# Whole float32 scores in the first twelve heads of an attention-and-mixer kernel, instead of the first eight

## The chip, the cores and the metric

The kernel runs on one core of one Trainium2 chip. The metric is device microseconds of one execution, the median of several. Five engines have queues of their own: PE (TensorE, matmuls), DVE (VectorE), ACT (ScalarE), POOL (GpSimd), and SP (SyncE), which here only issues DMAs. Each queue runs in order, so an instruction that waits holds up all behind it on its engine; engines meet through semaphores.

## The reference, cut to what matters

```python
# q, k, v: (8 batches, 8 heads, 576 tokens, 64), float32
scores = scale * np.matmul(q, k.transpose(0, 1, 3, 2))
scores = np.where(block_i >= block_j, scores, -1e9)      # blocks of 64 tokens
attn = softmax(scores)                                   # with 1e-9 added to the sum
x = attn @ v                                             # -> (8, 576, 512)
u = x + ((x.transpose(0, 2, 1) @ U) @ V).transpose(0, 2, 1)   # U: 576x32, V: 32x576
out = u + np.maximum(u @ w_ch1, 0.0) @ w_ch2             # 512 -> 2048 -> 512
```

The weights U, V, w_ch1 and w_ch2 are float64 and come as pairs of 32-bit words.

## The kernel before

**Stages.** The attention runs head by head, 64 heads (8 batches of 8), numbered 0 to 63. Two heads make a pair; after each pair `mix` projects the pair's columns through U and V, and after four pairs a batch's u is complete. The channel mixer is cut in two halves of 1024 hidden columns. The first half (`ffn_chunk`, 16 chunks of 288 tokens, L465 and L488) is laid between the heads' work wherever PE has room, and what is left of it runs after the last head. The second half (`block_products`, L659) runs after that, alone. The first two chunks belong to batch 0 and are run in two turns, since the second half of their weights comes later. A chunk needs its batch's u, and the weights w1 and w2 of the first half, which come in 16 pieces of 128x512.

**Float32 products.** Most matmuls split an operand into a float32r high part and a rest and multiply the parts. The scores of heads from FS on are made like this: `split_qk` fetches q and k into `raw` twice (rows 0 to 63 and 64 to 127), ACT makes q1 and k1 (high parts, L877 and L878), POOL subtracts for the rest of q (L880), DVE for the rest of k (L885), and a DMA copies the high part of q to the lower rows of q2 (L892). Each tile of scores is then two float32r matmuls, L935 (q1, k1) and L936 (q2, k2). Heads below FS fetch q and k once, ACT scales k in place (L874), and each tile of scores is one whole float32 matmul of `raw` (L931), which the profile records in two halves. Rows 64 to 127 of `raw` hold the block mask as a product of two constant matrices; for the split form DVE casts them into q2 and k2 at heads FS - 2 and FS - 1 (L867). A head has five tiles of scores, of 64, 192, 320, 448 and 576 keys (the last as two of 288, in the bank `bw`). After them come the maximum (L949, DVE), exponentials (L960, ACT), inverse sums (L976, L977, DVE), normalising (L986, POOL), transposes on PE (L1019), and the product with v (L1061 in heads below FP = 10, L1077 in split form from there on).

**Weights.** A weight piece is fetched (L372, L387), takes an absolute value on ACT (L353), four DVE instructions (L331, L332, L337, L345), a cast on ACT (L360) and a subtraction on POOL (L361).

**What sets the order.** `Plan` collects all work as tasks with an engine, a cost in ns, a priority and dependencies. `issue` walks a model of the five engines in time and, whenever an engine is free in the model, issues its ready task with the smallest priority. A head h has priorities around 1000 h, its `split_qk` 900 earlier than the head before, the mixer's matmuls 1,000,000 and more; the weight pieces have numbers that put them between certain heads. So a changed cost or task anywhere changes the order of everything behind it, on all engines. Semaphores then keep the program right whatever the real times are. The costs that the plan gives to a head's scores:

```python
        if h < FS:
            add("PE", sum(1.667 * n for n in ns) / 2, pr, products, [raw], [bank])
        else:
            add("PE", _pe(*ns, m=ms), pr, products, [q1, k1, q2, k2], [bank])
```

Of the kernel before, what the change touches and what calls it, by code (L numbers as in the profile page):

```python
# [43 lines left out]

FP = 10

FS = 8

PB = (1, 1, 1, 2, 2)

# [87 lines left out]
class Plan:  # L138
# [8 lines left out]
    def add(self, engine, ns, prio, fn, reads=(), writes=(), hold=(), after=0, port=False):  # L147

        n = len(self.tasks)
        deps = set()  # L150
        for b in reads:
            deps.update(b.writers)
            b.readers.append(n)
        for b in hold:
            deps.update(b.readers, b.writers)
        for b in writes:
            deps.update(b.readers, b.writers)
            b.writers, b.readers = [n], []
        deps.discard(n)
        slots = {b for b in (*reads, *writes) if b.pool is not None}  # L160
        for b in slots:
            b.users += 1
        self.tasks.append((engine, ns, prio, fn, deps, after, slots, port or engine == "POOL"))
# [91 lines left out]
def attention_then_mixer(  # L255
# [599 lines left out]
    def split_qk(h, pr):  # L855
        raw, q1, k1, q2, k2 = (r[h % 2] for r in (raw_r, q1_r, k1_r, q2_r, k2_r))

        def fetch():
            nc.sync.dma_start(out=raw[0:64, :], in_=qk[h])
            if h >= FS:  # L860
                nc.sync.dma_start(out=raw[64:P, :], in_=qk[h])

        if h in (FS - 2, FS - 1):

            for n, (x, o) in enumerate(((q2, 0), (k2, S))):
# [3 lines left out]
                )  # L869
        add("SP", 1640 if h >= FS else 820, pr, fetch, writes=[raw], after=DL)  # L870
        if h < FS:
            add(
# [36 lines left out]
    def softmax(h, tiles, pr):  # L909
# [14 lines left out]
        def products():  # L924
            for i, at in parts:
                qs = slice(P * i + 64 - (P if i else 64), P * i + 64)
                for j in range(2 if wide else 1):
                    o = bank[:, j, :T] if wide else view(i, at)
                    ks = slice(j * T, j * T + T) if wide else slice(0, P * i + 64)
                    if h < FS:  # L930
                        nc.tensor.matmul(  # L931
# [7 lines left out]
        for i in tiles:  # L939
            ns += [T] * 4 if wide else [P * i + 64] * 2  # L940
            ms += [P if i else 64] * (4 if wide else 2)
        if h < FS:
            add("PE", sum(1.667 * n for n in ns) / 2, pr, products, [raw], [bank])
# [294 lines left out]
```

## Time and profile before

| what | before |
|---|---|
| median of 3 runs | 1201.78 us (1198.8 to 1202.18) |
| the profiled execution's own time | 1201.04 us |
| its span, first to last instruction | 1199.2 us |
| mean granted TensorE clock | 0.996 |
| first head's scores | 5.3 us |
| first split scores (head 8) | 77.3 us |
| first mixer matmul (L465) | 103.5 us |
| projection of heads 14 and 15 | 198.7 and 199.7 us |
| last projection (heads 62 and 63) | 676.5 us |

The profile is of one execution. Busy times of engines are sums over instructions; on PE, a matmul's recorded time runs from its start to a modelled end and overlaps with the next one's, so what a matmul costs in a stream is the distance from its start to the next start.

### The profile page before, as it was taken

The numbers are of one execution on the slowest core, as the hardware profiler recorded it, in microseconds if no ns is written. First come the engines' busy times: TensorE is split into PE (matmuls) and PEld (weight loads), VectorE is DVE, ScalarE is ACT, GpSimd is POOL, SyncE is SP. The second block draws the span as 40 slices with busy tenths as digits, with TensorE's granted clock in tenths as the row PEclk, the third lists the DMA queues.
The fourth block names the chain that finished last, engine by engine and source line by source line (L and its number), as shares of the span: only waits on it lengthen the run. The fifth ranks groups of instructions, "written<-read, shape, count | busy, mean of one in ns | idle before, by whom it ended". The sixth has DMA issues, their size and how long they took to land.

```text
span 1199.2 us, 25106 instructions
## 1 busy us (share of the span) xinstructions
PE 1169.1 (97%) x8970; PEld 1123.6 (94%) x8970; DVE 980.7 (82%) x2061; ACT 734.0 (61%) x1822; POOL 426.3 (36%) x588
## 2 busy tenths in 40 slices
PE   7989998999999999999999999999999999999998
PEld 5657888999999999999999999999999999999998
DVE  6879899888988898888887488425989889889887
ACT  6878686777878787878786344213544544544443
POOL 4558766665656566665654112210000000000000
PEclk9999999999999999999999999999999999999999
DMA  4465656535364535354532343211231231231221
GB/s 127 146 172 155 188 166 166 139 97 156 81 171 108 144 104 153 101 158 106 144 98 70 104 147 111 81 54 49 72 119 49 72 119 49 72 119 60 60 80 40
DMA packets 76428, 132.13 MB, mean 110 GB/s; under 512 B 9040, under 2 KB 53072, under 8 KB 76304
## 3 DMA queue, kind: packets, MB, share of 16 engines
q1 hardware_dynamic: 76304, 130.53, 38.8%
q8 instruction: 71, 1.16, 0.4%
q14 instruction: 53, 0.43, 0.1%
HBM read 92.75 MB, written 29.49 MB: 102 GB/s over the span
## 4 chain that ended last, share of the span: by engine, by line
PE 79%; DVE 11%; ACT 4%; issue 2%; DMA 2%; SPq 0%; POOL 0%; ACTq 0%; DVEq 0%; POOLq 0%
PE bb L659 29%; PE bf L465 10%; PE bf L488 10%; PE ba L1019 7%; PE ba L1077 5%; PE bg L465 4%; PE bg L488 4%; DVE mx L949 2%; DVE pl L1038 2%; ACT p L960 2%; PE ba L935 2%; PE ba L936 2%; PE ba L1061 1%; PE ba L1116 1%; PE ba L1102 1%
## 5 line engine op out<-in xcount | busy, mean ns | idle before, releaser
L986 POOL TENSOR_SCALAR p<-p,rv 128x192 f32<-128x192 f32 (+4 forms) x320 | 181.0, 580 | 150.5 <-DVE rv L977 92.7
L659 PE MATMUL bb<-hh,w1l 128*128 128x288 f32 x704 | 170.1, 295 | 0.0
L659 PE MATMUL bb<-hh,w1h 128*128 128x288 f32 x704 | 169.4, 295 | 0.0
L960 ACT ACTIVATE p<-ba,mx 128x448 f32<-128x448 f32 (+3 forms) x248 | 114.3, 466 | 22.2 <-DVE mx L949 18.9
L1019 PE MATMUL ba<-ident,p 128*128 128x128 f32 x768 | 123.5, 275 | 2.2 <-DVE pw L994 0.7
L1038 DVE TENSOR_TENSOR pl<-ba,ph 128x512 fp32r<-128x512 f32 x216 | 114.0, 550 | 11.7 <-ACT ph L996 9.2
L659 PE MATMUL bb<-hl,w1h 128*128 128x288 f32 x576 | 123.0, 295 | 0.1
L659 PEld LDWEIGHTS bb<-hh,w1l 128*128 128x128 f32 x704 | 122.9, 190 | 0.0
L659 PEld LDWEIGHTS bb<-hh,w1h 128*128 128x128 f32 x704 | 121.9, 188 | 0.0
L488 PE MATMUL bf<-hh,w2h 128*128 128x288 f32 x392 | 121.2, 309 | 0.0
L488 PE MATMUL bf<-hl,w2h 128*128 128x288 f32 x392 | 116.4, 297 | 0.0
L488 PE MATMUL bf<-hh,w2l 128*128 128x288 f32 x392 | 115.6, 295 | 0.0
L996 ACT CAST ph<-ba 128x512 fp32r<-128x512 f32 x216 | 100.5, 493 | 23.1 <-PE ba L1019 18.3
L447 POOL TENSOR_TENSOR ul<-ur,uh 128x288 fp32r<-128x288 f32 x72 | 63.3, 907 | 129.7 <-PE bf L465 72.6
L613 ACT CAST hh<-hb 128x576 fp32r<-128x576 f32 x98 | 65.9, 672 | 60.6 <-PE bb L659 58.1
L949 DVE TENSOR_REDUCE mx<-ba 128x1 f32<-128x448 f32 (+3 forms) x248 | 94.1, 407 | 10.0 <-PE ba L936 5.4
L1019 PEld LDWEIGHTS ba<-ident,p 128*128 128x128 f32 x768 | 90.5, 141 | 7.9 <-issue 4.5
L880 POOL TENSOR_TENSOR q<-raw,q 64x576 fp32r<-64x576 f32 x56 | 82.6, 1475 | 29.1 <-issue 9.2
L659 PEld LDWEIGHTS bb<-hl,w1h 128*128 128x128 f32 x576 | 91.9, 188 | 0.4 <-DVE hl L614 0.4
L1077 PE MATMUL ba<-ph,vs 128*128 128x256 f32 (+3 forms) x432 | 90.7, 263 | 0.1
L465 PE MATMUL bf<-uh,w1l 128*128 128x288 f32 x392 | 80.8, 303 | 0.0
L488 PEld LDWEIGHTS bf<-hh,w2l 128*128 128x128 f32 x392 | 74.9, 191 | 0.2
(167 smaller groups left out, 3288.1 us busy)
## 6 DMA issues: line engine op xcount, KB each, us to landing
raw<-in_qk_dram SPq DMA_DIRECT2D x120, 288.0 KB, 4.4
st<-in_w_dram SPq DMA_DIRECT2D x32, 512.0 KB, 3.6
o_d<-ot SPq DMA_DIRECT2D x72, 144.0 KB, 2.1
vr<-in_v_dram SPq DMA_DIRECT2D x32, 320.0 KB, 3.4
ur<-u_d SPq DMA_DIRECT2D x64, 144.0 KB, 3.0
whole<-o_d SPq DMA_DIRECT2D x32, 288.0 KB, 3.2
out_dram<-whole SPq DMA_DIRECT2D x32, 288.0 KB, 2.2
ur<-u_d SPq DMA_DIRECT2D x30, 288.0 KB, 3.2
```

Source lines behind the costliest of these rows:

```text
L465: nc.tensor.matmul(ps[:, :T], w()[wn][:, k, fs], m[k].ap, start=(i == 0), stop=(i == len(ops) - 1))
L488: nc.tensor.matmul(ps[:, :T], w()[wn][:, f, ms], hs[f][x].ap, start=(i == 0), stop=(i == len(ops) - 1))
L613: add("ACT", _act(2 * T, True), E, lambda: nc.scalar.copy(h.ap, x[0]()), [x[1]], [h])
L659: nc.tensor.matmul(bank[:, i, :T], x()[:, w(k)], p.ap[:, k, :], start=first and n == 0, stop=last and n == len(ops) - 1)
L880: "POOL", 1380, pr, lambda: nc.gpsimd.tensor_sub(q1[64:P, :], raw[64:P, 0:S], f32(q1[64:P, :])),
L949: lambda i=i, at=at: nc.vector.tensor_reduce(out=mx[: P if i else 64, i : i + 1], in_=view(i, at), op=ALU.max, axis=AX.XY if wide else AX. ...
L960: nc.scalar.activation(out.rearrange("p (j k) -> p j k", j=2) if wide else out, view(i, at), AF.Exp, bias=mx[:rows, i : i + 1], accum_out= ...
L986: lambda x=x, rows=rows, i=i: nc.gpsimd.tensor_scalar(out=x, in0=x, scalar1=rv[:rows, i : i + 1], scalar2=1.0, op0=ALU.mult, op1=ALU.mult),
L996: add("ACT", _act(n), pr, lambda: nc.scalar.copy(out(), inp()), reads, writes)
L1019: nc.tensor.transpose(out=bank[:, a : a + P], in_=pt_r[i][h % PB[i]][:, j * P : (j + 1) * P], identity=perm.ap)
L1038: "DVE", _dve(m), pr, lambda: nc.vector.tensor_sub(pl[:, low], bank[:, :m], f32(ph[:, low])), [bank, bh], [bl]
L1077: nc.tensor.matmul(bank[0 : c.stop, a:n], vs[:, j, c], x[:, _at(g, j)], start=(i == 0), stop=(i == len(ops) - 1))
```

## The change

`FS`, the number of heads with whole float32 scores, goes from 8 to 12:

```diff
-FS = 8
+FS = 12
```

Heads 8 to 11 now take the branch `h < FS` in `split_qk` (one fetch, one ACT pass, nothing on POOL and DVE, no copy of q) and in `softmax` (five tiles of one whole float32 matmul each, the last one as two). The casts of the mask (L867) move from heads 6 and 7 to heads 10 and 11. The condition `h < 8` that picks the bank of the 448-key tile stays as it is. The tasks' costs change with the branch, and so the plan orders the program anew: PE has 3072 matmuls of the first mixer half in both, but 282 of them stood ahead of the second projection matmul of heads 14 and 15 before, and 312 now; ahead of the last projection 1860 before, and 1818 now.

On PE, the first mixer matmul and what stands just ahead of it, before (bank bf takes mixer products, ba scores and transposes; k_0, q_0 are the parts of head 10):

```order
L935 MATMUL ba_97<-k_0_147,q_0_145 128x320
L936 MATMUL ba_97<-k_0_128,q_0_126 128x320
L935 MATMUL ba_98<-k_0_147,q_0_145 128x192
L936 MATMUL ba_98<-k_0_128,q_0_126 128x192
L935 MATMUL ba_98<-k_0_147,q_0_145 64x64
L936 MATMUL ba_98<-k_0_128,q_0_126 64x64
L465 MATMUL bf_90<-uh_106,w1h_199 128x288
```

The same place now (p are a head's probabilities, xt a pair's columns):

```order
L1019 MATMUL ba_97<-swap,p_0_137 128x128
L1019 MATMUL ba_97<-ident,p_0_139 128x128
L1019 MATMUL ba_97<-ident,p_0_137 128x128
L1019 MATMUL ba_97<-ident,p_0_139 128x128 x2
L465 MATMUL bf_90<-uh_106,w1h_199 128x288
L465 MATMUL bf_90<-uh_107,w1h_199 128x288
```

The first mixer matmul has moved behind all of head 10's scores, the first two matmuls of head 11's, and transposes of probabilities that came after it before.

On DVE, the last step of the last of the 16 weight pieces (the L345 here), before (mx are maxima, ut the sums of a pair's projection):

```order
L1136 TENSOR_TENSOR ut_170<-ba_95,xt_163 128x288
L1045 TENSOR_TENSOR ph_158<-ba_98,ph_158 64x64
L331 TENSOR_SCALAR z_103<-z_103 128x512
L332 TENSOR_SCALAR z_103<-z_103 128x512
L1038 TENSOR_TENSOR pl_159<-ba_95,ph_157 128x256
L949 TENSOR_REDUCE mx_154<-bw 128x1
L337 SCALAR_TENSOR_TENSOR z_103<-st_101,z_103 128x512
L1085 TENSOR_TENSOR xt_164<-ba_98,tmp_161 64x256
L1038 TENSOR_TENSOR pl_159<-ba_95,ph_157 128x320
L345 SCALAR_TENSOR_TENSOR z_103<-st_101,z_103 128x512
```

And now:

```order
L1038 TENSOR_TENSOR pl_159<-ba_96,ph_157 128x256
L337 SCALAR_TENSOR_TENSOR z_103<-st_101,z_103 128x512
L1122 TENSOR_TENSOR t_0_167<-tz_168,t_0_167 32x128
L345 SCALAR_TENSOR_TENSOR z_103<-st_101,z_103 128x512
L1038 TENSOR_TENSOR pl_160<-ba_95,ph_158 128x512
L1085 TENSOR_TENSOR xt_164<-ba_96,tmp_162 64x320
L1136 TENSOR_TENSOR ut_170<-ba_98,xt_163 128x288
L1038 TENSOR_TENSOR pl_160<-ba_97,ph_158 128x448
```

The piece's last step was row 373 on DVE and is now row 345; it stood behind the projection sums (L1136) of heads 12 and 13 and stands ahead of them.

On SP, the first copy of q (L892) and its neighbours, before, for head 8 (u_d holds u, st a weight piece, vr v, in_qk the queries and keys):

```order
L387 DMA st_101<-in_w_dram 128x1024
L859 DMA raw_131<-in_qk_dram 64x1152
L861 DMA raw_131<-in_qk_dram 64x1152
L898 DMA vr_149<-in_v_dram 128x640
L372 DMA st_100<-in_w_dram 128x1024
L892 DMA q_0_126<-q_0_145 64x576
L859 DMA raw_130<-in_qk_dram 64x1152
```

And now, for head 12:

```order
L898 DMA vr_150<-in_v_dram 128x640
L387 DMA st_101<-in_w_dram 128x1024
L892 DMA q_0_126<-q_0_145 64x576
L859 DMA raw_130<-in_qk_dram 64x1152
L861 DMA raw_130<-in_qk_dram 64x1152
L859 DMA raw_131<-in_qk_dram 64x1152
```

The first copy has moved from head 8 to head 12; ahead of it stands one weight fetch and one of v, without the pair of fetches of the next head.

## Prediction

> **What bounds the kernel now.** I read the page first, then a table of windows by stage, then the instructions in order of time around the heads that change.
>
> The page's first lines and two of its slice lines (40 slices of 30 us):
>
> ```profile
> span 1199.2 us, 25106 instructions
> PE 1169.1 (97%) x8970; PEld 1123.6 (94%) x8970; DVE 980.7 (82%) x2061; ACT 734.0 (61%) x1822; POOL 426.3 (36%) x588
> PE   7989998999999999999999999999999999999998
> DVE  6879899888988898888887488425989889889887
> ```
>
> TensorE carries the kernel, but not evenly: it has gaps in the first seven slices, which is where heads 8 to 11 run. The windows, cut at the places I need (busy us of each engine, then the granted clock, DMA share, GB/s):
>
> ```profile
> 63.70:103.50 39.80, 33.24 (x205) 23.35 (x205) 30.70 (x66) 31.89 (x87) 24.77 (x29) 1.00 0.67 174
> 103.50:172.50 69.00, 65.34 (x517) 62.95 (x515) 64.28 (x147) 52.23 (x143) 49.23 (x61) 0.98 0.61 172
> 172.50:200.00 27.50, 22.20 (x157) 19.64 (x156) 25.83 (x60) 19.48 (x54) 18.13 (x24) 0.88 0.53 148
> 200.00:660.00 460.00, 457.05 (x3777) 445.67 (x3777) 391.76 (x1017) 360.16 (x1032) 277.18 (x397) 1.00 0.47 124
> 700.00:1150.00 450.00, 449.86 (x3389) 449.63 (x3388) 358.68 (x539) 186.92 (x306) 18.25 (x18) 1.00 0.27 82
> ```
>
> From 200 us on PE is idle 3 us in 460, and after the attention not at all; 450 us hold 3389 products of 288 columns, 0.133 us each. Between 63.7 and 200 us it is idle 6.6 + 3.7 + 5.3 = 15.5 us, and runs at half clock for 2% of 69 us and 12% of 27.5 us, which loses 1.4 + 3.3 = 4.7 us: 20.2 us in all. DVE is busy 93% and 94% of the second and third window. So whatever is done to PE after 200 us shows in full; up to there DVE shares the pace, and PE has some room.
>
> **Part 1: the added passes on PE.** Twelve rows give the price: first a head with whole scores, whose matmuls are recorded in halves, then a head with split scores. What counts is start to start, since records overlap.
>
> ```profile
> 53.93 1.14 PE L931 MATMUL bw<-raw 128*128 128x288 f32 x4
> 54.90 0.92 PE L931 MATMUL bf<-raw 128*128 128x448 f32 x2
> 55.65 0.27 PE L1102 MATMUL ba<-ident,xt 128*64 128x128 f32 x1
> 59.76 1.29 PE L931 MATMUL ba<-raw 128*128 128x320 f32 x6
> 60.98 0.44 PE L1019 MATMUL ba<-swap,p 128*128 128x128 f32 x2
> ...
> 99.66 0.30 PE L935 MATMUL bw<-k,q 128*128 128x288 f32 x1
> 99.79 0.30 PE L936 MATMUL bw<-k,q 128*128 128x288 f32 x1
> 99.92 0.30 PE L935 MATMUL bw<-k,q 128*128 128x288 f32 x1
> 100.06 0.29 PE L936 MATMUL bw<-k,q 128*128 128x288 f32 x1
> ...
> 102.44 0.47 PE L935 MATMUL ba<-k,q 128*128 128x448 f32 x1
> 103.48 0.22 PE L936 MATMUL ba<-k,q 128*64 128x64 f32 x1
> 103.54 0.77 PE L465 MATMUL bf<-uh,w1h 128*128 128x288 f32 x4
> ```
>
> Whole: 54.90 - 53.93 = 0.97, 55.65 - 54.90 = 0.75, 60.98 - 59.76 = 1.22, together 2.94 us. Split: four at 0.133 = 0.53, and 103.54 - 102.44 = 1.10, together 1.63 us. The change adds 1.31 us a head, 5.2 us for four heads. All of it falls before about 112 us.
>
> **Part 2: what goes away beside PE.** Rows of 70 to 120 us, and one row of the whole run (last):
>
> ```profile
> L880 POOL TENSOR_TENSOR q<-raw,q 64x576 fp32r<-64x576 f32 x5 | 8.1, 1615 | 0.5 <-POOL p L986 0.2
> L885 DVE SCALAR_TENSOR_TENSOR k<-raw,k 64x576 fp32r<-64x576 f32 x5 | 5.5, 1103 | 0.7 <-ACT k L878 0.6
> L877 ACT CAST q<-raw 128x576 fp32r<-128x576 f32 x6 | 4.0, 672 | 0.1
> L337 DVE SCALAR_TENSOR_TENSOR z<-st,z 128x512 int32<-128x512 int32 x4 | 4.5, 1132 | 0.0
> L337 DVE SCALAR_TENSOR_TENSOR z<-st,z 128x512 int32<-128x512 int32 x32 | 24.1, 756 | 0.3
> ```
>
> Each of four heads loses one DVE subtraction (4 x 1.10 = 4.4 us), one POOL subtraction (4 x 1.62 = 6.5), one of two ACT passes (4 x 0.67 = 2.7), a second fetch and the copy of q. DVE is the fullest, so its saving is the one that can move time; what of it arrives where is worked out in part 4. POOL (49 of 69 us busy) and ACT (52 of 69) have room: nothing counted.
>
> Row L337 runs 1132 ns here against 756 overall. The Trainium skill (SBUF — State Buffer, "Who interferes with whom") has a reason: a VectorE instruction with two SBUF inputs and a GpSimd one that reads SBUF block each other on a shared port. By it the fewer POOL subtractions would speed DVE further: four times 0.38 us is 1.5 us, and the sum would end 1.5 us lower. I leave it out, since other POOL work keeps that port busy too.
>
> **Part 3: a wait that moves.** The first split head has a stall of its own:
>
> ```profile
> 72.34 0.49 SPq L892 DMA_DIRECT2D q<-q  x1
> 77.30 0.38 PE L935 MATMUL bw<-k,q 128*128 128x288 f32 x1
> 80.82 0.40 PE L936 MATMUL bw<-k,q 128*128 128x288 f32 x1 [3.14 <-DMA q<-q]
> DMA to landing us min/median/max: 2.3/3.7/8.4
> ```
>
> The copy of q issued at 72.3 lands 8.4 us later, and PE stands 3.1 us with everything queued behind it. Now head 12 is first. Its copy again stands on SP's queue behind a 512 KB weight fetch, with fewer 288 KB fetches around it. Bounds: nothing returns (gain 3.1) or all returns; I take half, a gain of 1.6 us. The price if it all returns stands in the range.
>
> Moved at equal cost: four casts on DVE, from heads 6 and 7 to heads 10 and 11.
>
> ```profile
> L867 DVE CAST q<-raw x2: 685/1029/1373, 32.9 to 41.2; 64x576 fp32r<-64x576 f32 x2
> L867 DVE CAST k<-raw x2: 452/986/1521, 33.5 to 42.5; 64x576 fp32r<-64x576 f32 x2
> ACT raw L874 <- DMA raw<-in_qk_dram: 6.0, 4, 2.4
> ```
>
> And raw is held until PE has read it, so four more fetches wait for PE; the first eight heads had four waits of ACT on such a fetch, 2.4 us at most. Four more lie between 0 and 9.6 us on ACT; I take 0, as ACT has 17 us idle in 69.
>
> **Part 4: where the saving ends.** Filler (the first mixer half, L465 and L488) starts at 103.54. Until batch 1's attention is projected and the second half of w2 is split, only two token chunks of it can run. The places:
>
> ```profile
> 187.89 1.82 POOL L361 TENSOR_TENSOR w2l<-z,w2h 128x512 fp32r<-128x512 f32 x1 [0.16 <-ACT w2h L360]
> 199.74 0.40 PE L1131 MATMUL ba<-v,t 96*128 96x288 f32 x1
> 676.47 0.43 PE L1131 MATMUL ba<-v,t 96*128 96x288 f32 x2
> ```
>
> The last piece of w2 is ready at 189.7; PE is emptiest between 172.5 and 200 because filler has run short. In the new order the last DVE step of that piece is row 345, not 373, so filler should not run out for so long.
>
> Now two marks. At the projection at 199.74 (heads 14 and 15) DVE has 172.0 us of work behind it in the new order and 172.6 in the old (medians of its forms, summed in order); the four subtractions, whose median is 0.74, really took 1.10 each, 1.4 us more. So DVE reaches the mark 0.6 + 1.4 = 2.0 us of work earlier, 2.2 us at 93% busy; with the 1.6 of part 3, 3.8 us. The rest of the saving is not lost: it went into other work that now stands ahead of the mark, and PE has 312 filler products behind it there instead of 282, 30 x 0.133 = 4.0 us. At the last projection (676.47) DVE has 3.9 us less by medians, 5.3 with the 1.4, 6.2 us of time at the 85% of the 460 us window; with the 1.6, 7.8 us. But 1818 filler products stand ahead of it, not 1860: 42 x 0.133 = 5.6 us are left for afterwards, at PE's full rate.
>
> Two ends for the sum. If PE sets the pace from the first mark on, the end comes 3.8 + 4.0 = 7.8 us earlier: 1194.0. The added 5.2 us are inside, since the mark is a place in an order that holds them; but PE must do 5.2 + 4.0 us more in 3.8 us less, so 13.0 of the 20.2 us lost must vanish. If DVE sets the pace of the attention to its end, the sum is 7.8 - 5.6 = 2.2 us earlier: 1199.6. The window 200 to 660 (PE 457 of 460 busy, DVE 392) speaks for the first, the 13.0 us that must vanish against its full size. I take the middle, 5.0 us earlier.
>
> The profiled execution took 1201.04 us, 1.8 beside its span and 0.7 below the median 1201.78. From 1201.04 the sum gives 1196.0; against the median, as the two ends above, 1196.8, which I forecast.
>
> **Rivals.** Slower: PE is already the pace from 103.5 us (65.3 of 69 busy). By the new order, with the spacings above, 82.0 us of attention matmuls stand ahead of the first filler product instead of 74.6, 7.4 us more. If that product starts after 103.5 + 7.4 = 110.9 us, the gaps before it have absorbed nothing, and the 5.2 us come in full: 1207.0. For it speaks that DVE is only 77% busy up to 103.5, so its saving may not be what PE waits for there; against it, that PE has 6.6 us of idle time in just that stretch.
>
> Same: the attention is paced by DVE to its end, 1199.6 as above. For it: DVE 392 of 460 us busy, with short waits in every head; against it, PE 457.
>
> More: the gap at 172.5 to 200 closes whole and the half clock goes with it, 4.7 us beside the 7.8: 1189.3, and 1188 if the other half of the 3.1 us stall goes too. The granted clock falls to 0.88 just where PE has least to do. The Trainium skill (TensorE: Matmul & The Clock Gate, "The HAM clock gate") says that an idle window of about 3.4 us halves PE's clock; by that rule closing the gaps returns the 4.7 us, and a stall at head 12 that outlasts such a window would cost another, 1.7 us. The trace agrees so far.
>
> That the scores stay as they were is excluded: the new order has the whole form in four more heads.
>
> **How the numbers follow.** A measurement of this kernel tells about 0.3% (3.6 us) from no change. The middle case, 1192 to 1198.2: 0.36. More, below 1192: 0.15. Same, 1198.2 to 1205.4: 0.30. Slower: 0.19. So faster 0.51. The range 1188 to 1206 leaves out some 0.04 below and 0.16 above, holds both ends of the sum, and takes in a stall at head 12 that returns whole (1.6 us on top of either); the likeliest case's own range is 1192 to 1198.
>
> **What would show it.** Right: 144 records of L931 instead of 96, 2.9 us a head; the first L465 at or before 105 us; the stall on the copy of q at head 12, under 3 us; the second L1131 of heads 14 and 15 near 194 to 198; PE's idle time between 63.7 and that mark under 9 us, and a clock above 0.95 there; 200 to 660 us as full as now. Wrong: the first L465 beyond 111 us, or PE's idle time after 200 us growing by more than the 5.0 us I gain.

## The result and the profile after

The changed kernel took 1192.43 us, median of 5 runs (1191.97 to 1196.2), against 1201.85 for the kernel before (5 runs, 1198.8 to 1203.87): ratio 0.9932, 95% interval 0.991 to 0.9954, so faster by 0.7%. The forecast was 1196.8, range 1188 to 1206. The profiled execution of the kernel after took 1194.45 us, 1.85 beside its span and 2.0 above its median; three of the other runs had spans of 1190.2 to 1190.6 us at a mean granted clock of 0.999 to 1.0, the profiled one 0.997. The profiled spans differ by 6.6 us.

The page's first lines after, and the slice lines of TensorE and VectorE:

```profile
span 1192.6 us, 25089 instructions
PE 1170.8 (98%) x8970; PEld 1122.8 (94%) x8970; DVE 967.8 (81%) x2057; ACT 732.3 (61%) x1818; POOL 413.5 (35%) x584
PE   7989999999999999999999999999999999999998
DVE  6877989888788888888887587216989889889887
```

The windows after, at the same places up to 660 us (start:end, length, busy us of PE, PEld, DVE, ACT and POOL with instruction counts, granted clock, DMA share, GB/s):

```profile
63.70:103.50 39.80, 35.84 (x197) 23.75 (x195) 32.08 (x73) 30.33 (x83) 21.53 (x29) 0.96 0.47 141
103.50:172.50 69.00, 65.81 (x507) 62.26 (x506) 61.41 (x143) 51.28 (x140) 43.26 (x56) 0.98 0.62 173
172.50:200.00 27.50, 27.45 (x222) 26.52 (x222) 26.11 (x67) 22.28 (x65) 19.59 (x26) 1.00 0.58 169
200.00:660.00 460.00, 456.18 (x3771) 443.92 (x3770) 389.01 (x1015) 359.64 (x1033) 274.98 (x396) 1.00 0.45 122
```

The change shows in one place above all. From 172.5 to 200 us TensorE was busy 22.20 us at clock 0.88; now it is 27.45 at 1.00. Between 63.7 and 200 us its idle time fell from 15.5 to 4.0 + 3.2 + 0.1 = 7.2 us, and what the lower clock costs (the window's length times what its mean clock lacks to 1.00) from 4.7 to 1.6 + 1.4 = 3.0. After 200 us little differs: 0.9 us more idle time in 460.

The instructions that the prediction named, in order of time, after (start us, busy us, engine, line):

```profile
107.77 0.77 PE L465 MATMUL bf<-uh,w1h 128*128 128x288 f32 x4
...
172.54 1.29 POOL L361 TENSOR_TENSOR w2l<-z,w2h 128x512 fp32r<-128x512 f32 x1
175.91 0.29 PE L488 MATMUL bf<-hh,w2h 128*128 128x288 f32 x1
...
187.54 0.64 PE L465 MATMUL bf<-uh,w1h 128*128 128x288 f32 x3
...
195.81 0.64 PE L1131 MATMUL ba<-v,t 96*128 96x288 f32 x2
...
664.34 0.43 PE L1131 MATMUL ba<-v,t 96*128 96x288 f32 x2
```

Read them against the kernel before. The last piece of w2 is ready at 173.8 instead of 189.7. Filler (mixer matmuls) comes in turns of 96 products, half L465 and half L488; the third turn is the first that multiplies the last four pieces of w2. In the kernel before, its L488 stopped after the twelve products of the first two of those pieces:

```profile
174.74 0.30 PE L488 MATMUL bf<-hl,w2h 128*128 128x288 f32 x1
...
190.02 0.38 PE L488 MATMUL bf<-hh,w2h 128*128 128x288 f32 x1
```

No filler ran in those 15 us, and it went on 0.3 us after the last piece was ready. Now the third turn's L488 start at 175.91, when all four pieces are there, and follow the L465 with no such hole. The fourth turn starts at 187.54, where it started at 201.2. The second projection of heads 14 and 15 stands at 196.1 instead of 199.74, the last of all 12.1 us earlier. But the first filler product is 4.2 us later, at 107.77.

Of VectorE's work on weight pieces between 70 and 120 us, before (the L337 row stands in the prediction) and then after, as the groups by line show it:

```profile
L332 DVE TENSOR_SCALAR z<-z 128x512 int32<-128x512 int32 x4 | 3.9, 974 | 0.1
L345 DVE SCALAR_TENSOR_TENSOR z<-st,z 128x512 int32<-128x512 int32 x4 | 3.3, 830 | 0.0
L331 DVE TENSOR_SCALAR z<-z 128x512 f32<-128x512 f32 x4 | 1.8, 451 | 0.0
```

```profile
L345 DVE SCALAR_TENSOR_TENSOR z<-st,z 128x512 int32<-128x512 int32 x6 | 5.7, 951 | 0.0
L337 DVE SCALAR_TENSOR_TENSOR z<-st,z 128x512 int32<-128x512 int32 x5 | 3.4, 675 | 0.0
L331 DVE TENSOR_SCALAR z<-z 128x512 f32<-128x512 f32 x5 | 3.1, 621 | 1.2 <-ACT z L353 1.2
L332 DVE TENSOR_SCALAR z<-z 128x512 int32<-128x512 int32 x5 | 3.1, 617 | 0.2
L885 DVE SCALAR_TENSOR_TENSOR k<-raw,k 64x576 fp32r<-64x576 f32 x1 | 0.7, 740 | 0.0
```

The four steps of a piece took 1132 + 974 + 830 + 451 = 3387 ns before and 675 + 617 + 951 + 621 = 2864 after: 0.52 us less for the same four steps, though two of them (L345 and L331) take longer. The subtraction (L885) is there once instead of five times.

### The profile page after: what moved, and what is told of

It is laid out like the page before. It is cut to its first block, busy times and chain, and to the rows that moved or that the text cites. A ratio compares the mean times of both kernels' runs of the same rounds, so it can differ in the third digit from the quotient of the medians.

```text
span 1192.6 us, 25089 instructions
## 1 busy us (share of the span) xinstructions
PE 1170.8 (98%) x8970; PEld 1122.8 (94%) x8970; DVE 967.8 (81%) x2057; ACT 732.3 (61%) x1818; POOL 413.5 (35%) x584
## 4 chain that ended last, share of the span: by engine, by line
PE 61%; DVE 4%; issue 1%; ACT 1%; DMA 1%; POOL 0%; DVEq 0%; ACTq 0%; POOLq 0%
PE bb L659 29%; PE bf L465 7%; PE bf L488 6%; PE bg L488 5%; PE bg L465 4%; PE ba L1019 3%; PE ba L1077 3%; PE ba L936 1%; PE ba L935 1%; PE ba L1116 1%; DVE mx L949 1%; PE ba L1102 1%; PE bw L935 1%; DVE pl L1038 1%; PE bw L936 1%
## 5 line engine op out<-in xcount | busy, mean ns | idle before, releaser
L986 POOL TENSOR_SCALAR p<-p,rv 128x192 f32<-128x192 f32 (+4 forms) x320 | 178.6, 573 | 153.0 <-DVE rv L977 84.0
L960 ACT ACTIVATE p<-ba,mx 128x448 f32<-128x448 f32 (+2 forms) x248 | 114.5, 466 | 23.6 <-DVE mx L949 22.1
L488 PE MATMUL bf<-hh,w2h 128*128 128x288 f32 x376 | 117.2, 312 | 0.0
L488 PE MATMUL bf<-hl,w2h 128*128 128x288 f32 x376 | 111.5, 297 | 0.0
L488 PE MATMUL bf<-hh,w2l 128*128 128x288 f32 x376 | 110.9, 295 | 0.0
L447 POOL TENSOR_TENSOR ul<-ur,uh 128x288 fp32r<-128x288 f32 x72 | 59.8, 858 | 131.8 <-PE bg L465 109.8
L880 POOL TENSOR_TENSOR q<-raw,q 64x576 fp32r<-64x576 f32 x52 | 76.5, 1471 | 28.3 <-issue 11.2
L465 PE MATMUL bf<-uh,w1l 128*128 128x288 f32 x392 | 80.8, 303 | 0.0
L1077 PEld LDWEIGHTS ba<-ph,vs 128*128 128x128 f32 x432 | 73.2, 189 | 2.2 <-DVE xt L1085 0.6
```

Of the source, the lines that this page charges most:

```text
L465: nc.tensor.matmul(ps[:, :T], w()[wn][:, k, fs], m[k].ap, start=(i == 0), stop=(i == len(ops) - 1))
L488: nc.tensor.matmul(ps[:, :T], w()[wn][:, f, ms], hs[f][x].ap, start=(i == 0), stop=(i == len(ops) - 1))
L880: "POOL", 1380, pr, lambda: nc.gpsimd.tensor_sub(q1[64:P, :], raw[64:P, 0:S], f32(q1[64:P, :])),
L960: nc.scalar.activation(out.rearrange("p (j k) -> p j k", j=2) if wide else out, view(i, at), AF.Exp, bias=mx[:rows, i : i + 1], accum_out= ...
L986: lambda x=x, rows=rows, i=i: nc.gpsimd.tensor_scalar(out=x, in0=x, scalar1=rv[:rows, i : i + 1], scalar2=1.0, op0=ALU.mult, op1=ALU.mult),
L1077: nc.tensor.matmul(bank[0 : c.stop, a:n], vs[:, j, c], x[:, _at(g, j)], start=(i == 0), stop=(i == len(ops) - 1))
```

## Experiments

Two questions: does the gain come from the lighter work, from the new order of the program, or only from both; and which place in the program gives it. All ratios are against the kernel before in the same session (medians 1199.9 to 1200.5 us).

**1. The work without the order.** The kernel before, in its own order; in heads 8 to 11 the subtractions, the second fetch and the copy of q are left out, and the scores are one float32 product. It leaves out the rests of q and k in those four heads (ScalarE's rounded copies are what is multiplied).

```diff
+        whole = FS <= h < 12
...
-            if h >= FS:
+            if h >= 12:
...
-            "POOL", 1380, pr, lambda: nc.gpsimd.tensor_sub(...)
+            "POOL", 1380, pr, lambda: None if whole else nc.gpsimd.tensor_sub(...)
...
+                    if h < 12:
+                        nc.tensor.matmul(o, f32(q1[:, qs]), f32(k1[:, ks]), start=True, stop=True)
```

> The order of before on every engine, with the work of the change in heads 8 to 11: one fetch, no POOL and DVE subtraction, no copy of q, whole float32 matmuls (ACT keeps both passes; the operands are the rounded high parts, so the scores of these four heads leave out the rest of q and k). Theory 'lighter': the work taken off DVE, POOL and the DMA queue pays in the early stage, and PE takes the added 5.2 us into its idle time: 1194 to 1198, with no stall on the copy of q at 77 us. Rival 'order': what pays is the new order, and in the old one the added passes only cost: 1202 to 1207.

Measured 1200.63 us, ratio 1.0004 (0.9993 to 1.0016): no gain, and no loss either, between the two expected ranges. Its windows:

```profile
63.70:103.50 39.80, 37.61 (x215) 25.21 (x214) 26.86 (x67) 32.83 (x91) 18.82 (x28) 1.00 0.50 145
172.50:200.00 27.50, 22.88 (x150) 20.07 (x149) 25.59 (x58) 18.73 (x54) 17.60 (x23) 0.81 0.52 147
```

Ahead of 103.5 us the added passes are absorbed, as the prediction hoped (PE 37.61 busy against 33.24). But the hole at 172.5 to 200 stays, 22.88 us at clock 0.81: nothing brought the weight pieces forward, since the order is written ahead (the last is ready at 188.7).

**2. The order without the work.** The kernel after in its own order, but heads 8 to 11 split as before: the old steps are issued shortly after the step that replaced them.

```diff
+        def scale():
...
+            nc.scalar.copy(q1.ap, raw[:, 0:S])
+            nc.scalar.activation(k1.ap, raw[:, S : 2 * S], AF.Copy, scale=SCALE)
+            plan.put(700, lambda: nc.gpsimd.tensor_sub(q1[64:P, :], ...))
+            plan.put(701, lambda: nc.sync.dma_start(out=f32(q2[0:64, :]), ...))
+            plan.put(1300, lambda: nc.vector.scalar_tensor_tensor(out=k2[0:64, :], ...))
```

> The order of the change, with the work of before in heads 8 to 11: two fetches, both ACT passes, both subtractions, the copy of q and split float32r matmuls. Theory 'lighter': DVE and POOL are late again, filler starts later or runs short, 1197 to 1203, though PE has 5.2 us less to do. Rival 'order': the new order pays by itself, and with 5.2 us less on PE the time falls to 1187 to 1191.

Measured 1206.08 us, ratio 1.0048 (1.0031 to 1.0066): slower, and above both expected ranges. Windows, and TensorE's waits from 63.7 to 103.5 us (us in total, times, longest; in this kernel L966 and L965 are the split score products, L892 GpSimd's subtraction):

```profile
63.70:103.50 39.80, 28.94 (x157) 20.80 (x157) 30.92 (x61) 24.94 (x66) 20.79 (x24) 0.83 0.61 165
103.50:172.50 69.00, 62.36 (x448) 56.85 (x447) 61.17 (x133) 49.57 (x138) 43.87 (x58) 0.93 0.57 159
172.50:200.00 27.50, 26.96 (x221) 26.13 (x220) 24.29 (x59) 22.13 (x59) 20.13 (x25) 1.00 0.65 186
```

```profile
PE bw L966 <- DMA q<-q: 4.9, 2, 3.0
PE bw L965 <- POOL q L892: 3.6, 2, 2.7
```

The new order closes the hole here too (26.96 of 27.5), but it follows each fetch with the scores almost at once. The split needs ScalarE, GpSimd and a DMA in between, so TensorE waits 8.5 us for them ahead of 103.5 us, at clock 0.83. Part of that wait is the experiment's own, since the plan that wrote this order knew nothing of the put-back steps. So neither half of this change gains by itself; another order with the old work can (experiment 5).

**3. What added TensorE work costs in a fixed order.** The kernel before, with the split scores of heads 8 to 11 done twice: 4 x 1.63 = 6.5 us more on TensorE, nothing else.

```diff
+                    for _ in range(2 if h < 12 else 1):
                         nc.tensor.matmul(o, q1[:, qs], k1[:, ks], start=True, stop=False)
                         nc.tensor.matmul(o, q2[:, qs], k2[:, ks], start=False, stop=True)
```

> Before, same order, with the split scores of heads 8 to 11 done twice on PE, 4 x 1.63 = 6.5 us more PE work and nothing else. Theory 'PE has room': its idle time between 63.7 and 200 us takes most of it, at most 3 us longer: 1202 to 1205. Rival 'PE is the pace': all of it shows, 1207 to 1209.

Measured 1204.95 us, ratio 1.0045 (1.0027 to 1.0062), 5.4 us slower (3.2 to 7.4 by the interval): about five sixths of the added work shows, between what the two theories expected. Between 63.7 and 200 us TensorE's idle time fell by only 2.6 us (15.5 to 12.9); it is no free room by itself.

**4. The stall of head 8.** The kernel before, with head 8's copy of q made by ScalarE from the fetched q instead of by a DMA.

```diff
+            if h == 8:
+                nc.scalar.copy(q2[0:64, :], raw[0:64, 0:S])
```

> Before, same order, with the copy of q for head 8 made by ACT from raw in place of the DMA, so that PE does not stand 3.1 us at 77 us. Theory 'stall': that wait is on the path and its loss shows at the end, 1198 to 1199.5. Rival 'hidden': what follows waits for DVE anyway, 1201 to 1202.5.

Measured 1200.2 us, ratio 0.9997 (0.9985 to 1.001). The 3.1 us stall is not told from worth nothing (the interval leaves a gain of 1.8 us at most): the first filler comes 1.4 us earlier (102.1), TensorE is busy 1.5 us longer up to 103.5 us, and from 172.5 to 200 us it is busy 1.0 us less:

```profile
172.50:200.00 27.50, 21.16 (x153) 18.71 (x152) 26.54 (x58) 19.04 (x54) 17.47 (x22) 0.94 0.54 152
```

**5. The weight pieces alone, in the kernel before.** One number: the priority of the last four pieces of w2. The scores stay as before.

```diff
-WP2, WP3, WP4 = 9000.0, 1000.0, 13000.0
+WP2, WP3, WP4 = 9000.0, 1000.0, 11000.0
```

> The kernel before (eight heads) with the priority of the last four pieces of w2 moved from 13000 to 11000, nothing else: their last step on VectorE then stands 13 rows ahead of the projection of heads 14 and 15 instead of 9 rows behind it. Theory H, what the change gained is the hole of TensorE at 172.5 to 200 us, which is there because filler waits for those pieces: the hole closes (TensorE over 26 of 27.5 us) and the time is 1191 to 1196 us without any change in the scores. Theory R, only the lighter work of four heads pays for the earlier pieces: the pieces push the attention back by what they cost, the hole moves ahead of 172.5 us, 1199 to 1204 us.

Measured 1195.74 us, ratio 0.9958 (0.9943 to 0.9973): 5.0 us faster without a changed score. Its window, and the last piece:

```profile
172.50:200.00 27.50, 25.85 (x198) 24.56 (x197) 25.94 (x63) 18.00 (x52) 16.14 (x21) 0.94 0.62 179
```

```profile
176.20 1.26 POOL L361 TENSOR_TENSOR w2l<-z,w2h 128x512 fp32r<-128x512 f32 x1 [1.14 <-ACT w2h L360]
```

The piece is ready 12.2 us earlier than in the kernel before and the hole is mostly closed (25.85, where the expectation asked for over 26).

**6. The weight pieces late, in the kernel after.** The opposite, 13000 to 15000, with twelve whole heads.

```diff
-WP2, WP3, WP4 = 9000.0, 1000.0, 13000.0
+WP2, WP3, WP4 = 9000.0, 1000.0, 15000.0
```

> The kernel after (twelve heads) with the priority of the last four pieces of w2 moved from 13000 to 15000: their last step on VectorE stands at row 390, at the projection of heads 14 and 15, as in the kernel before, instead of row 345. Theory H: the hole at 172.5 to 200 us opens again and the gain is lost, 1199 to 1203 us. Theory R: VectorE has the same work to the mark, the attention is a little earlier, 1191 to 1196 us.

Measured 1202.12 us, ratio 1.0009 (0.9996 to 1.0023): the whole gain is gone, 0.77% or 9.2 us above the kernel after.

```profile
103.50:172.50 69.00, 68.90 (x553) 66.08 (x552) 62.48 (x158) 56.30 (x157) 45.80 (x60) 1.00 0.65 181
172.50:200.00 27.50, 19.76 (x123) 17.77 (x122) 23.79 (x54) 18.45 (x53) 16.31 (x24) 0.81 0.46 134
```

```profile
187.78 1.27 POOL L361 TENSOR_TENSOR w2l<-z,w2h 128x512 fp32r<-128x512 f32 x1
...
208.73 0.69 PE L465 MATMUL bf<-uh,w1h 128*128 128x288 f32 x4
```

TensorE is full up to 172.5 us (68.90 of 69) and then starves: 19.76 of 27.5 at clock 0.81, the last piece ready at 189.05, no filler from 176.9 to 198.4, and the fourth turn at 208.73. After 200 us it is idle 7.6 us in 460, against 3.8. With experiment 5 this shows the place: the hole in the filler, set by when those pieces are planned, carries most of the change's gain, 5.0 of 8.2 us when it is closed by itself. How the rest divides is not shown, since a moved priority also reorders everything behind it.

**7. Which relief pays for it.** Three kernels: the kernel after in its own order, with the removed subtractions of heads 8 to 11 issued again and read by nobody: both, VectorE's alone, GpSimd's alone. The plan does not know of them.

```diff
+            if h >= 8:
+                plan.put(700, lambda: nc.gpsimd.tensor_sub(q1[64:P, :], raw[64:P, 0:S], raw[64:P, S : 2 * S]))
+                plan.put(1300, lambda: nc.vector.scalar_tensor_tensor(out=k2[0:64, :], ...))
```

> The kernel after, in its own order, with the removed subtractions of heads 8 to 11 issued again on VectorE (4 x 1.10 us) and GpSimd (4 x 1.62 us); what they write is read by nobody. Theory A, VectorE and GpSimd pace this order ahead of the mark: 4 to 6 us of the gain is lost, 1197 to 1199 us. Theory C, the DMA of q and ScalarE's saved pass were what mattered: 1192 to 1194 us. Theory B, the order carries it: 1192 to 1194 us too, and C and B are then told apart by the order of twelve heads with the work of eight, already measured at 1206 us, which speaks against B.

> The kernel after in its own order, with only VectorE's removed subtraction of heads 8 to 11 issued again (4 x 0.8 to 1.1 us; what it writes is read by nobody). With both put back the time was 1200.1 us against 1192.4, while one VectorE pass of the weight split (five of 128x512 float32 between 63.7 and 103.5 us) went from 703 to 1695 ns. Theory V, VectorE's own work paces: most of the loss, 1196 to 1199 us. Theory P, it is GpSimd's instructions that stand in VectorE's way on their common port: 1192 to 1195 us, with that pass near 703 ns.

> The same with only GpSimd's removed subtraction issued again (4 x 1.6 us), unread. Theory P: most of the loss without any more work on VectorE, 1196 to 1200 us, and the VectorE pass of the weight split above 1200 ns between 63.7 and 103.5 us. Theory V: 1192 to 1194 us, since GpSimd is busy only 21.5 of 39.8 us there.

Measured: both 1200.09 us, ratio 0.9992 (0.998 to 1.0004); VectorE's alone 1196.15, 0.9955 (0.9938 to 0.9972); GpSimd's alone 1198.1, 0.9977 (0.9966 to 0.9988). Against the kernel after's 0.9932 that is 0.60%, 0.23% and 0.45%: 7.2, 2.8 and 5.4 us. The interval of VectorE's alone overlaps that of the kernel after (0.991 to 0.9954), so its 2.8 us are no firm loss; the other two lie clear of it. The hole from 172.5 to 200 us stays closed in all three (27.3 of 27.5); the loss lies ahead of it. Windows from 63.7 to 103.5 us, VectorE's alone and then GpSimd's alone:

```profile
63.70:103.50 39.80, 34.28 (x183) 22.95 (x181) 35.62 (x73) 28.33 (x77) 20.49 (x27) 0.91 0.44 135
```

```profile
63.70:103.50 39.80, 33.14 (x174) 22.01 (x173) 35.58 (x68) 26.54 (x74) 22.20 (x25) 0.88 0.41 125
```

GpSimd's subtraction raises VectorE's busy time from 32.08 to 35.58 us, with five instructions fewer. Where that comes from, in the groups by line in that window: the kernel after, and the kernel with GpSimd's subtraction (where the same line is L343):

```profile
L332 DVE TENSOR_SCALAR z<-z 128x512 int32<-128x512 int32 x5 | 3.4, 680 | 0.2
```

```profile
L343 DVE TENSOR_SCALAR z<-z 128x512 int32<-128x512 int32 x6 | 7.8, 1300 | 0.2
```

And one of the six in order of time, with GpSimd's own instructions around it:

```profile
97.13 2.22 POOL L1004 TENSOR_SCALAR p<-p,rv 64x64 f32<-64x64 f32 x3
99.32 1.25 POOL L372 TENSOR_TENSOR w1l<-z,w1h 128x512 fp32r<-128x512 f32 x1
100.55 0.45 POOL L920 TENSOR_SCALAR vs<-vr 128x320 fp32r<-128x320 f32 x1
...
97.95 3.33 DVE L343 TENSOR_SCALAR z<-z 128x512 int32<-128x512 int32 x1
```

A step that takes 0.43 us elsewhere in that window lasts 3.33 us, from inside one GpSimd instruction to 0.3 us after the end of the last of an unbroken row of them (101.0). None of that row is a put-back subtraction; one of those runs just ahead of it (95.62 to 97.03). In the kernel after the same step begins at 95.54, while GpSimd is idle up to 95.91, and takes 0.43 us. TensorE then waits 2.9 us for the VectorE work behind the long step; over the window, in the kernel with GpSimd's subtraction, its longest entry is

```profile
PE ba L1037 <- DVE tz L1138: 4.4, 2, 2.9
```

against 0.5 for the same wait in the kernel after, and neither list has a wait for GpSimd itself. So by these waits GpSimd's own lateness is not what costs the time there. In the kernel before the plan holds the two engines apart, as its code does not start such a VectorE step beside a GpSimd task; there, the four removed GpSimd tasks take such slots away from the weight steps. That this is how the planner got the pieces forward is argued from its code; removing only those tasks from the plan was not tried.

**8. Other numbers of heads.** Ten, fourteen and sixteen whole heads, each with its own order.

> Ten heads with whole scores: half of the change, with its own order. Theory A, relief by amount (each head's lighter DVE and POOL work lets the planner bring weights and filler products forward, and the gain goes with the number of heads): half of the 9.4 us, so 1195 to 1198 us. Theory B, the particular order of twelve heads happens to suit the chip: any value between 1190 and 1206, with no half-way.

> Fourteen heads. Heads 12 and 13 lie in the part from 110 to 160 us, where TensorE in the kernel after is busy to about 95%, so each added pass of 1.31 us has less idle time to take. Theory A, relief by amount: 1188 to 1191 us as long as idle time is left ahead of the mark, with an end to the gain at about 1191 once TensorE's work paces (2 heads x 1.31 us = +2.6 us of TensorE, nothing to give back). Theory B: any value between 1190 and 1206.

> Sixteen heads. Theory A with the end of the gain: 1190 to 1198 us, since 4 x 1.31 = 5.2 us of further TensorE work meets under 8 us of idle time ahead of 200 us. Theory A without that end: 1184 us. Theory B: any value between 1190 and 1206.

Measured: ten 1191.74 us, ratio 0.9924 (0.9908 to 0.9941); fourteen 1201.09, 1.0 (0.9988 to 1.0012); sixteen 1195.84, 0.9956 (0.9942 to 0.9971). There is no gain by the head: ten do what twelve do (not told apart), and fourteen do nothing, where theory A asked for 1188 to 1191. The windows at 172.5 us of ten and sixteen, then four windows of fourteen:

```profile
172.50:200.00 27.50, 26.59 (x217) 26.06 (x218) 23.40 (x61) 19.18 (x56) 16.88 (x25) 1.00 0.52 147
```

```profile
172.50:200.00 27.50, 27.14 (x221) 26.42 (x220) 24.34 (x62) 22.96 (x66) 19.35 (x27) 1.00 0.69 184
```

```profile
63.70:103.50 39.80, 35.24 (x199) 23.01 (x198) 32.98 (x76) 30.10 (x83) 20.39 (x28) 1.00 0.44 132
103.50:172.50 69.00, 64.45 (x485) 58.05 (x483) 63.56 (x151) 52.97 (x148) 47.77 (x62) 1.00 0.57 161
172.50:200.00 27.50, 26.52 (x210) 24.82 (x209) 25.60 (x58) 19.83 (x57) 15.19 (x21) 1.00 0.62 169
200.00:660.00 460.00, 455.56 (x3754) 442.13 (x3753) 391.86 (x1009) 357.90 (x1027) 273.36 (x394) 1.00 0.45 122
```

All three close the hole (26.5 to 27.1 of 27.5), and by the rows of L931 each head past ten should add its 1.31 us on TensorE. Fourteen also has 0.6 + 1.4 + 0.9 + 0.6 = 3.5 us more idle time than twelve in these windows, which with 2 x 1.31 = 2.6 us makes 6.1 us; but its clock is 1.00 where the kernel after loses 3.0 us, so that 3.1 of the 7.4 us between the spans (1200.0 against 1192.6) are accounted for. Its last piece of w2 is ready at 179.9, later than twelve's (173.8), while ten's comes at 165.3 and sixteen's at 154.8. Whether that is the cause, and where the rest lies, stays open; theory A, a gain by the number of heads, is refuted.

## Why the prediction was right, and where it was not

The sign and the place were right, and the time lies in the range; the size was 4.4 us short against the median, 1.6 between the profiled spans (5.0 forecast, 6.6 found). That 5.0 was the middle between two ends, and the range of 18 us holds both, so the time lying in it is weak support; the marks say more.

**The marks (part 4).** Right. The projection of heads 14 and 15 moved by 3.6 us (3.8 forecast) with 312 filler products ahead of it instead of 282, as counted. The last projection moved 12.1 us with 42 fewer filler products ahead, 5.6 us, which leaves 6.5. So the first end, TensorE pacing from the mark on (-7.8), was nearly the whole answer, and the middle that I took was the mis-sized step: the second end, VectorE pacing to the end (-2.2), did not take place. TensorE's idle time after 200 us grew by only 0.9 us. Of the "13.0 us that must vanish" 10.9 are found: 10.0 between 63.7 and 200 us, and TensorE is busy 0.9 us longer ahead of it, 57.11 against 56.25; the rest I can't place by fixed windows.

**The reason given for it (filler short of w2).** Right: the rows of L488 show it directly, and experiments 5 and 6 from both sides. The prediction gave it as a reason and put no number to it.

**The added passes (part 1).** The price held (the first four halves of one head still take 104.28 - 103.30 = 0.98 us in the rows of L931 after). That TensorE "has some room" was wrong as a reason: in a fixed order 5.4 of 6.5 us show. That VectorE's and GpSimd's lighter work pays for them in the change is argued from experiment 1, where the two just cancel (1.0004).

**The removed work beside TensorE (part 2).** Mis-sized: part 4 counts only VectorE's own saving, whose loss alone is not firm in experiment 7 (2.8 us), and "POOL and ACT have room: nothing counted" puts at nothing the subtractions that cost 5.4 us there. (That is what they cost when put back into the new order unplanned; what their absence gave the change was not measured by itself.) The 1.5 us that I worked out and then left out were there: 0.52 us less per piece, 2.6 us over five pieces between 70 and 120 us. The Trainium skill (SBUF — State Buffer, "Who interferes with whom") says that GpSimd and some VectorE instructions lock each other out of a shared port for a whole instruction. The 3.33 us above agree that a VectorE step can be held up wholly, but it was held up through several GpSimd instructions in a row, not one.

**The stall of head 8 (part 3).** Probably wrong in size: I counted 1.6 us, and experiment 4 found nothing (0.9997), though its interval reaches 1.8; 1.0 of the 1.5 us that TensorE had gained by 103.5 us is missing again in the hole at 172.5 us. No stall came back at head 12: TensorE has no wait on that copy after. That the mark's 3.8 came out at 3.6 is then partly luck: the 1.6 us here and the weight steps' 2.6 us left out are errors of opposite sign, and with both put right the sum would be 4.8.

**The rivals.** More came nearest: the hole closed whole and the median run has a clock of 0.999. Its 1189.3 holds the 1.6 us of the stall; reckoned afterwards, without it 1190.9, and 0.9 us of new idle time after 200 us makes 1191.8, against 1192.4. The profiled execution kept 3.0 of the 4.7 us that the lower clock cost. Slower did not decide: its first filler product at 110.9 was not reached, but 107.77 is past the 105 that I named as right. That sign was a poor one: a first filler at 102.1 (experiments 1 and 4) gains nothing, and one at 101.63 (ten heads) gains 0.76%.

**The signs.** L931 has 144 records; idle time between 63.7 and the mark is 7.2 us (under 9); the clock there is 0.96 to 1.00 (above 0.95).

**The clock.** Two readings of the prediction don't hold. The clock column is a mean, so 0.98 and 0.88 say that 2% and 12% were lost, not that TensorE ran at half clock for that share of the time; the 4.7 us stand. And "The trace agrees so far" holds for the halving, but not for the length of an idle stretch: in the kernel before, the stall of 3.1 us at 77 us left the clock at 1.00, while it was 0.50 from 178.4 to 185.1 us, with only two gaps of 0.6 and 0.7 us in the 3 us ahead of it.

## What to carry to other kernels

Where a planner writes the order, a change of work is first a change of order: read which late piece the waiting engine starves for, here the last four of sixteen weight pieces, and try moving those by themselves, as one priority gave 5.0 us without the change, which gave 8.2 (0.68%). An idle engine is not free room: in a fixed order about five sixths of the added TensorE work showed. Work on an engine that is half idle can still be dear, if it holds up a busy engine beside it, as GpSimd's four subtractions cost 5.4 us in experiment 7.

## What the runs showed of the hardware

A VectorE step of 0.43 us on 128x512 int32 lasted 3.33 us beside GpSimd instructions that followed one another without a gap, and the mean of such steps between 63.7 and 103.5 us went from 680 ns (five) to 1300 ns (six) with four more GpSimd subtractions in the program.

In the windows where TensorE had gaps its granted clock went down with them: 0.81 with 7.7 us idle in 27.5, 0.83 with 10.9 in 39.8, 1.00 with 0.1 in 27.5. But it does not follow the sum of the gaps alone: from 63.7 to 103.5 us it was 1.00 with 6.6 us idle in the kernel before and with 4.6 us at fourteen heads, and 0.96 with 4.0 us in the kernel after. In shorter windows of 1.7 us it is seen to drop to 0.50: in the kernel before from 123.9 to 125.6 us, behind a gap of 1.7 us, where products stand 0.24 us apart instead of 0.133.
